# A whole second Strassen level in the first down product, and the snapshots' additions moved from VectorE to ScalarE and GpSimd

## The chip, the cores and the metric

The kernel runs on one core of one Trainium2 chip. The metric is device time in microseconds (us), the median of several runs. One further execution was taken by the hardware profiler; "the profile" and "the trace" are of that execution. The engines are named as in the profile: PE is TensorE's matrix multiplication, PEld its weight load, DVE is VectorE, ACT is ScalarE, POOL is GpSimd, SP is SyncE, which issues most of the transfers.

## What is computed

A transformer block on 2048 tokens of 1024 values, in bf16: linear attention with 32 heads of 32, then a feed-forward network with a ReLU gate. Both work on a normalised input and are added to what came in.

```python
h  = x  + linear_attention(layernorm(x), wqkv, wo)      # wqkv 1024 x 3072, wo 1024 x 1024
n  = layernorm(h)
gate = n @ W_gate                                       # 1024 x 3584
up   = n @ W_up                                         # 1024 x 3584
h2 = h + ((gate * (gate > 0)) * up) @ W_down            # 3584 x 1024
```

## The kernel before

**Order of the work.** The program text does not issue instructions. An object `Plan` records every operation, with the parts of memory that it reads and writes, and then sorts the operations of each engine by a list schedule with fixed costs and due times (`schedule`); the result is one fixed order per engine. Each engine works its own queue in order and waits at an instruction whose inputs are not ready, with everything behind it. As all operations are issued by one line (`call` in `Plan.take`, line 122), every row of the profile shows L122, and operations are told apart by shapes and times.

**Strassen products.** The large products are done in the Strassen-Winograd form: a product of 2 x 2 blocks takes seven block products instead of eight, with sums of the blocks made on DVE beforehand and additions of partial results afterwards. `Quad` holds one such set of seven. It has three PSUM banks A, D and E. `p1` writes A, and a `fork` (an ACT copy from PSUM to PSUM) puts the same into D. `p6` is added to A, and a first snapshot `u2` of A is taken; `p5` goes to E; `p7` is added to A, and a second snapshot `u3` is taken; `p2` is added to D, which gives the result c11, and E with u3 gives c22; later `p4` on A gives c21, and `p3` on E, with u2, gives c12. `Quads.run` interleaves neighbours: the order on PE is p1, then p4 and p3 of the quad before, then p6, p5, p7, p2. So p3 writes bank E again after c22 has been read from it.

**The stages.** Attention comes first. Then the gate and up products with a first Strassen level (`gu_quad`, matmuls of 512 columns in pairs of banks); their results are the left matrices of the down product, partly kept in SBUF, partly spilled to DRAM (`l_dram`, `s_dram`). Sums of `W_down`'s blocks are made meanwhile and spilled to `r_dram` (`wd_sums`).

**The down stage** begins at 573.44 us. Its outer Strassen level has seven products m, done in the order 1, 2, 6, 5, 7, 3, 4; each product is 1024 tokens by 1792 by 512. `deep` does a product through a second, inner level: two quads, one for each half g of the tokens, each with seven inner products. An inner product has 2 token tiles x 7 steps = 14 matmuls of 256 columns. For this `inner_rights` makes four sums of the weights (t1, t2, t4, t3) and `inner_lefts` four sums of the left matrix for each g (s1, s2, s4, s3), DVE operations of 128x1792 in fp16. They are put into rings of fixed places in SBUF (`inner_r`, `inner_l`, in KB per partition). The quads use five banks, 0 to 4 (`deep_banks`).

The first product, m=1, is different in the kernel before: only half g=1 goes through the inner level. Half g=0 is done by `shallow`: plain accumulation over 14 steps with matmuls of 512 columns, four blocks in banks 5 to 7, each copied by ACT into the running results `UM`. Its right matrix `r1` is loaded during the gate stage in two halves of 896 KB (k = 0 and 1), and its left matrix `z1` in two pieces.

**Where results go.** `begin` starts the running results U from m=1. `plus` adds a product to a running result: it serves m=2, 6, 5, 3 and 4, ten quads in all. Its `usnap` takes both snapshots of the quad by one DVE addition straight from PSUM: bank A plus the running result goes to the new running result. `both`, for m=7, takes plain snapshots (`plain_snap`, an ACT copy to a scratch place from `m_ring`) and updates two running results, ten DVE additions for each quad. Finished parts are stored by POOL's queue, which adds them to what `out` already holds, or at the very end by SP's queue.

The functions that the change touches, and what calls them:

Of the kernel before, what the change touches and what calls it, by code (L numbers as in the profile page):

```python
# [9 lines left out]
ALU = mybir.AluOpType  # L10
FP32 = mybir.dt.float32
BF16 = mybir.dt.bfloat16
FP16 = mybir.dt.float16
# [435 lines left out]
def ring_of(items):  # L449
    n = [0]  # L450

    def take():
        n[0] += 1
        return items[(n[0] - 1) % len(items)]

    return take
# [3 lines left out]
def block_kernel(ctx: ExitStack, tc: tile.TileContext, x, wqkv, wo, wg, wu, wd, out, H: int):  # L460
    nc = tc.nc
    P = 128
# [11 lines left out]
    FH = FC // 2  # L474
# [24 lines left out]
    def at(kb, shape, dt=BF16):  # L499
        n = 1  # L500
        for v in shape:
            n *= v
        size = n * (2 if dt == FP32 else 1)
        lo = int(kb * KB)
        assert lo == kb * KB and lo + size <= MEM, (kb, shape)
        a = mem[:, lo:lo + size]
        if dt != BF16:
            a = a.bitcast(dt)
        if len(shape) == 2:
            a = a.rearrange("p (a b) -> p a b", b=shape[1])  # L510
        elif len(shape) == 3:
            a = a.rearrange("p (a b c) -> p a b c", b=shape[1], c=shape[2])
        elif len(shape) == 5:
            a = a.rearrange("p (a b c d e) -> p a b c d e", b=shape[1], c=shape[2], d=shape[3], e=shape[4])
        elif len(shape) == 4:
            a = a.rearrange("p (a b c d) -> p a b c d", b=shape[1], c=shape[2], d=shape[3])
        return a
# [15 lines left out]
    def bank(b, n=1):  # L533
        return psum[:, b, :] if n == 1 else psum[:, b:b + n, :]
# [13 lines left out]
    hw, nc = nc, Plan(nc)  # L548
# [219 lines left out]
    def v_quad(p):  # L768
        v = v_ring()

        def blk(i, j):
            return v[:, i, j * KH:(j + 1) * KH, 0:P]

        def copy(i, j):
            return lambda ps: nc.scalar.copy(out=blk(i, j), in_=split(ps))

        def add(i, j):
            return lambda ps, u: nc.vector.tensor_tensor(out=blk(i, j), in0=split(ps), in1=split(u), op=ALU.add)

        return v, Quad(tok_prod(p, WV), fork, snap,  # L780
                       {"c11": copy(0, 0), "c12": add(0, 1), "c21": copy(1, 0), "c22": add(1, 1)}, five_banks)
# [86 lines left out]
    for p in range(1, NP):  # L868
# [9 lines left out]
        v, vq = v_quad(p)  # L878
# [77 lines left out]
    o_ring = ring_of([at(180 + SH + 2 * i, [D]) for i in range(2)])  # L956
# [231 lines left out]
    order = [(0, fc) for fc in range(4)] + [(1, fc) for fc in (2, 3, 0, 1)]  # L1188
# [15 lines left out]
    DW = D // 2  # L1204
    DQ = D // 4
    FQ = FH // 2
# [22 lines left out]
    for n, (s, fc) in enumerate(order):  # L1229
# [18 lines left out]
        if n == 24:  # L1248
            r1 = at(164, [2, FQ, DW])
            for k in range(2):  # L1250
                nc.sync.dma_start(out=r1[:, k, :, :], in_=wd_pairs[:, 0, :, k, 0:DW])
            z1 = l1_part(0, 12)
# [8 lines left out]
    lq = [at(84, [FQ, 4, 2, SW])[:, :, q, :, :] for q in range(4)]  # L1261
# [1 line left out]
    lx = at(0, [FQ, 2, SW], FP16)  # L1263
    L0 = {1: lq[0], 2: lq[1], 3: lf[1], 4: lq[3], 5: lx, 6: lf[0], 7: lf[2]}
    z_kb, r_kb = ring_of([14, 28]), ring_of([42, 164])
    inner_r, inner_l = ring_of([150.5, 178]), ring_of([0] + [140, 72] * 6)
    h_ring = ring_of([i for i in range(4)])
    o_ring = ring_of([190.5 + i for i in range(7)])
    m_ring = ring_of([197.5 + 2 * i for i in range(3)])
    UM = at(56, [NS, 2, 2, 2, DQ], FP32)  # L1270
    of_v = of.rearrange("(t p) d -> p t d", p=P)
    deep_banks = five([bank(b) for b in range(5)])
    shallow_bank = ring_of([bank(b) for b in (5, 6, 7)])

    def U(s, v, g):
        return UM[:, s, g, v, :, :]

    def Y(s, v, g):
        n = (2 * s + v) * 2 + g
        return at(84 + 8 * n if n < 7 else 188.5, [2, DQ], FP32)  # L1280

    def add(o, x, y):
        nc.vector.tensor_tensor(out=o, in0=x, in1=y, op=ALU.add)

    def pair(a):
        return a.rearrange("p (t d) -> p t d", t=2)
# [12 lines left out]
    def store(q, s, tt, lo, width, o, onto_h):  # L1299

        t = tile_no(q, s, tt)
        lo += q % 2 * DW
        dst = of_v[:, t:t + o.shape[1], lo:lo + width]
        if onto_h:
            nc.gpsimd.dma_start(out=dst, in_=o, accum_op=ALU.add)
        else:
            nc.sync.dma_start(out=dst, in_=o)
# [21 lines left out]
        for f in range(FQ):  # L1329
            nc.sync.dma_start(out=L0[m][:, f, :, :], in_=s_dram[m][:, 2 * f:2 * f + 2, :])  # L1330

    def shallow(m, r, lefts, order, then, tts=range(4)):
        for s in order:
            for tt in tts:
                b = shallow_bank()
                for f in range(FH):
                    if f == FH - 1:
                        nc.cut()
                    nc.tensor.matmul(b, lhsT=lefts[s][f][:, tt * P:(tt + 1) * P], rhs=r[:, f % 2, f // 2, :],
                                     start=(f == 0), stop=(f == FH - 1), skip_group_check=True)  # L1340
                then(s, tt, b)

    def inner_rights(r):
        y = [[r[:, k, :, v * DQ:(v + 1) * DQ] for v in range(2)] for k in range(2)]
        kb = inner_r()
        t1, t2, t4 = (at(kb + 3.5 * i, [FQ, DQ], FP16) for i in range(3))
        t3 = y[0][1] if r.dtype == FP16 else None
        if t3 is None:
            t3 = y[0][1].bitcast(FP16)
        for o, a, b in ((t1, y[0][1], y[0][0]), (t2, y[1][1], t1), (t4, y[1][0], t2), (t3, y[1][1], y[0][1])):  # L1350
            nc.vector.tensor_tensor(out=o, in0=a, in1=b, op=ALU.subtract)
        return y[0][0], y[1][0], y[1][1], t4, t1, t2, t3
# [26 lines left out]

        return of(x00), of(x01), of(s4), x11, of(s1), of(s2), s3.get  # L1380

    def deep(m, r, x1, outs, gs=range(2)):

        rights = inner_rights(r)

        def quad(g):
            lefts = inner_lefts(L0[m], x1[g], g)

            def prod(ps, k, start):
                for tt in range(2):  # L1390
                    for f in range(FQ):
                        nc.tensor.matmul(ps[:, tt * DQ:(tt + 1) * DQ], lhsT=lefts[k - 1](f)[:, tt * P:(tt + 1) * P],
                                         rhs=rights[k - 1][:, f, :], start=(start and tt == 0 and f == 0),
                                         stop=(f == FQ - 1), skip_group_check=True)

            usnap, end = outs(g)
            return Quad(prod, fork, usnap, {
                "c11": lambda D: end(0, 0, D, None), "c21": lambda A: end(1, 0, A, None),
                "c12": lambda E, u: end(0, 1, E, u), "c22": lambda E, u: end(1, 1, E, u)}, deep_banks)

        for g in gs:
            quads.run(quad(g))

    def plus(src, dst=None, q=None, last=False):


        def outs(g):
            with_h = last and g == 1

            def base(s, v):  # L1410
                x = src(s, v, g)
                if with_h:
                    add(x, x, load_h(q, s, 2 * g, 2, v * DQ, DQ))
                return x

            def usnap(A, which):
                b = base(which, 1)
                o = dst(which, 1, g)
                add(o, pair(A), b)
                return o  # L1420

            def end(s, v, ps, u):
                x = base(s, v) if u is None else u
                if q is None:
                    add(dst(s, v, g), pair(ps), x)
                else:
                    o = at(o_ring(), [2, DQ])
                    add(o, pair(ps), x)
                    store(q, s, 2 * g, v * DQ, DQ, o, not with_h)

            return usnap, end

        return outs

    def plain_snap(A, which):
        u = scratch_u()
        nc.scalar.copy(out=u, in_=pair(A))
        return u

    def seven(s, tt, b):  # L1440
        for v in range(2):
            y = U(s, v, tt // 2)[:, tt % 2, :]
            add(y, b[:, v * DQ:(v + 1) * DQ], y)
        o = at(o_ring(), [1, DW])
        for v in range(2):
            c = slice(v * DQ, (v + 1) * DQ)
            add(o[:, 0, c], b[:, c], Y(s, v, tt // 2)[:, tt % 2, :])
        store(3, s, tt, 0, DW, o, True)

    def begin(g):  # L1450

# [28 lines left out]
    def step(m, outs):  # L1480
        deep(m, right(m), left(m), outs)


    shallow(1, r1, ([lq[0][:, f // 2, f % 2, :] for f in range(FH)], [z[:, f, :] for z in z1 for f in range(z.shape[1])]), (1, 0),
            lambda s, tt, b: nc.scalar.copy(out=UM[:, s, 0, :, tt, :], in_=b.rearrange("p (v d) -> p v d", v=2)), (0, 1))
    z1 = [z.rearrange("p (j u) t -> p u j t", u=2)[:, :, :, 2 * P:] for z in z1]
    deep(1, r1, {1: [(lo, lo + z.shape[2], z[:, 0, :, :], z[:, 1, :, :]) for lo, z in zip((0, 6), z1)]}, begin, (1,))

    step(2, plus(U, scratch_u, q=0))
    left0(5)  # L1490

# [5 lines left out]
    r, z = right(7), left(7)  # L1497
    deep(7, r, z, both)

    o_ring = ring_of([*(4 + i for i in range(10)), *(190.5 + i for i in range(7))])  # L1500
# [54 lines left out]
```

## Time and profile before

| | us |
|---|---|
| median of 3 runs | 730.73 (730.35 to 730.91) |
| profiled execution, its own time | 730.03 |
| its span in the trace | 728.2 |
| start of the down stage on PE | 573.44 |
| end of the last matmul | 724.78 |
| busy in the span: PE | 715.6 |
| DVE | 557.7 |
| ACT | 278.8 |
| POOL | 80.3 |

The span runs from the first to the last event in the trace; 1.83 us of the profiled execution lie around it. Matrix products fill the span almost wholly: PE is busy for 98% of it. After the last matmul a single addition and a store of 1.81 us follow. Times in the trace are counted from the start of the span.

### The profile page before, as it was taken

What the parts mean: (1) busy time and instruction counts of PE and PEld (TensorE: products, weight loads), DVE (VectorE), ACT (ScalarE), POOL (GpSimd) and SP (SyncE); (2) the same over time, 40 slices, a digit from 0 to 9 for tenths busy, and PEclk for the clock granted to TensorE, in tenths of its full rate; (3) what the DMA queues carried; (4) which work ended last, traced back from release to release, by engine and by line L of the source; (5) the groups of instructions that cost most, each with busy time, mean ns of one, the idle gap of its engine ahead of it and who ended that gap; (6) DMA issues with size and microseconds to landing.
All of it is one profiled execution on the core that took longest, in us unless ns stands there. A gap on an engine that the chain in (4) does not pass through costs nothing.

```text
span 728.2 us, 11123 instructions
## 1 busy us (share of the span) xinstructions
PE 715.6 (98%) x4121; PEld 391.7 (54%) x4121; DVE 557.7 (77%) x941; ACT 278.8 (38%) x543; POOL 80.3 (11%) x90
## 2 busy tenths in 40 slices
PE   8999999999999999999999999999999999999998
PEld 3444545444444444444444444444444488888887
DVE  6997635896897785575767969769766869899996
ACT  5778545666555443333333333333333220001100
POOL 2433000002202120000000000000000004101452
PEclk9999999999999999999999999999999999999999
DMA  9955205239946730456156485675591878867974
GB/s 308 240 125 115 38 1 173 60 84 239 198 102 151 143 83 1 123 145 181 58 145 200 151 252 159 190 242 186 161 292 59 287 244 222 247 223 230 246 81 61
DMA packets 156503, 117.40 MB, mean 161 GB/s; under 512 B 54944, under 2 KB 140192, under 8 KB 156320
## 3 DMA queue, kind: packets, MB, share of 16 engines
q1 hardware_dynamic: 148832, 113.01, 54.5%
q0 software_dynamic: 7616, 3.67, 4.9%
q8 instruction: 32, 0.52, 0.3%
q14 instruction: 23, 0.19, 0.1%
HBM read 70.52 MB, written 34.08 MB: 144 GB/s over the span
## 4 chain that ended last, share of the span: by engine, by line
PE 86%; DVE 5%; ACT 3%; DMA 3%; issue 1%; POOL 0%; SPq 0%; ACTq 0%; DVEq 0%
PE psum L122 86%; DVE mem L122 4%; ACT mem L122 3%; DMA mem<-mem 3%; DVE tiny L122 1%; POOL mem L122 0%; DMA mem<-in_A_x_dram 0%; ACT tiny L122 0%; SPq L122 0%; ACT psum L122 0%; ACTq L122 0%; DVEq L122 0%
## 5 line engine op out<-in xcount | busy, mean ns | idle before, releaser
L122 PE MATMUL psum<-mem 128*128 128x512 f16 (+4 forms) x4105 | 714.5, 337 | 7.9 <-ACT mem L122 3.5
L122 PEld LDWEIGHTS <-mem 128*128 128x128 f16 (+1 forms) x4121 | 391.7, 98 | 332.8 <-issue 8.2
L122 DVE TENSOR_TENSOR mem<-psum,mem 128x512 f32<-128x512 f32 (+2 forms) x238 | 186.0, 794 | 108.9 <-ACT mem L122 71.1
L122 DVE TENSOR_TENSOR mem<-mem 128x512 f16<-128x512 bf16 (+8 forms) x394 | 237.1, 642 | 13.5 <-DMA mem<-mem 8.1
L122 ACT COPY mem<-psum 128x512 f32<-128x512 f32 (+2 forms) x124 | 92.6, 749 | 216.7 <-PE psum L122 212.8
L122 ACT COPY psum<-psum 128x512 f32<-128x512 f32 (+1 forms) x67 | 48.5, 725 | 157.6 <-PE psum L122 143.2
L122 POOL DMA_DIRECT2D out_dram<-mem x28 | 34.1, 1299 | 415.1 <-DVE mem L122 415.0
L122 POOL TENSOR_SCALAR mem<-mem,tiny 128x1024 bf16<-128x1024 bf16 x30 | 39.6, 1320 | 196.5 <-ACT tiny L122 174.0
L122 ACT ACTIVATE mem<-psum 128x512 bf16<-128x512 f32 x90 | 53.8, 598 | 16.9 <-PE psum L122 16.3
L122 DVE SCALAR_TENSOR_TENSOR mem<-mem 128x512 bf16<-128x512 bf16 (+1 forms) x71 | 58.6, 825 | 1.4
L122 DVE SCALAR_TENSOR_TENSOR mem<-psum,mem 128x512 bf16<-128x512 f32 x66 | 45.3, 688 | 11.9 <-PE psum L122 7.9
L122 ACT ACTIVATE mem<-mem,tiny 128x1024 bf16<-128x1024 bf16 x25 | 28.6, 1145 | 10.8 <-issue 4.7
L122 DVE TENSOR_SCALAR mem<-mem 128x512 bf16<-128x512 bf16 (+1 forms) x49 | 16.4, 334 | 20.8 <-ACT mem L122 20.6
L122 ACT ACTIVATE mem<-mem 128x1024 bf16<-128x1024 f32 (+1 forms) x24 | 25.3, 1055 | 5.9 <-DVE mem L122 5.9
L122 DVE TENSOR_TENSOR mem<-psum,tiny 128x384 bf16<-128x384 f32 (+1 forms) x48 | 22.9, 508 | 5.3 <-ACT tiny L122 3.9
L122 ACT ACTIVATE tiny<-tiny 128x1 f32<-128x1 f32 (+2 forms) x112 | 22.7, 206 | 9.1 <-DVE tiny L122 6.2
L122 ACT ACTIVATE tiny<-psum 128x12 f32<-128x12 f32 (+1 forms) x48 | 8.1, 169 | 13.8 <-PE psum L122 13.4
L122 ACT CAST mem<-psum 128x512 bf16<-128x512 f32 x18 | 10.5, 581 | 2.9 <-PE psum L122 2.2
L122 DVE BATCH_NORM_STATS2 tiny<-mem 128x6 f32<-128x512 bf16 x14 | 9.0, 678 | 2.4 <-DMA mem<-in_A_x_dram 2.4
L122 POOL TENSOR_SCALAR tiny<-tiny 128x1 f32<-128x1 f32 x14 | 5.1, 367 | 25.7 <-ACT mem L122 18.1
L122 ACT ACTIVATION_READ_ACCUMULATOR mem<-mem,tiny 128x1 f32 x25 | 4.7, 189 | 0.0
L122 DVE TENSOR_SCALAR tiny<-tiny 128x1 f32<-128x1 f32 x16 | 3.4, 210 | 0.3
(18 smaller groups left out, 13.5 us busy)
## 6 DMA issues: line engine op xcount, KB each, us to landing
l_dram<-mem SPq DMA_DIRECT2D x98, 128.0 KB, 2.2
mem<-l_dram SPq DMA_DIRECT2D x12, 896.0 KB, 6.5
mem<-in_A_x_dram SPq DMA_DIRECT2D x32, 256.0 KB, 3.0
mem<-in_B_W_up_dram SPq DMA_DIRECT2D x14, 512.0 KB, 5.2
mem<-in_B_W_gate_dram SPq DMA_DIRECT2D x14, 512.0 KB, 4.3
mem<-in_B_W_down_dram SPq DMA_DIRECT2D x28, 256.0 KB, 3.7
r_dram<-mem SPq DMA_DIRECT2D x56, 128.0 KB, 2.0
mem<-r_dram SPq DMA_DIRECT2D x8, 896.0 KB, 5.5
```

The costliest lines, as they stand in the source:

```text
L122: call = lambda: getattr(getattr(self.nc, eng), op)(*args, **k)
```

## The change

The half g=0 of the product m=1 goes through `deep` like the others, so that `shallow`, its banks and the unused function `seven` are gone, and `deep` loses its parameter for the halves. For this product the sums of the right matrix get their own three places in SBUF (188, 196 and 199.5 KB), which are free before the gate stage ends, and those of the left matrix a place more in their ring. The scratch ring `m_ring` lies elsewhere during m=1.

Independent of that, `usnap` in `plus` now takes each snapshot in two steps: an ACT copy from PSUM to a scratch place, and a POOL addition of that copy and the running result. There are 20 such snapshots.

```diff
-    inner_r, inner_l = ring_of([150.5, 178]), ring_of([0] + [140, 72] * 6)
+    inner_r = ring_of([(188, 196, 199.5)] + [tuple(kb + 3.5 * i for i in range(3)) for kb in (150.5, 178)] * 3)
+    inner_l = ring_of([0, 140, 0, 72] + [140, 72] * 5)
...
-    m_ring = ring_of([197.5 + 2 * i for i in range(3)])
+    m_ring = ring_of([178, 180, 182, 184])
...
-    shallow_bank = ring_of([bank(b) for b in (5, 6, 7)])
...
-    def shallow(m, r, lefts, order, then, tts=range(4)):
-        for s in order:
-            for tt in tts:
-                b = shallow_bank()
-                for f in range(FH):
-                    if f == FH - 1:
-                        nc.cut()
-                    nc.tensor.matmul(b, lhsT=lefts[s][f][:, tt * P:(tt + 1) * P], rhs=r[:, f % 2, f // 2, :],
-                                     start=(f == 0), stop=(f == FH - 1), skip_group_check=True)
-                then(s, tt, b)
-
     def inner_rights(r):
         y = [[r[:, k, :, v * DQ:(v + 1) * DQ] for v in range(2)] for k in range(2)]
-        kb = inner_r()
-        t1, t2, t4 = (at(kb + 3.5 * i, [FQ, DQ], FP16) for i in range(3))
+        t1, t2, t4 = (at(kb, [FQ, DQ], FP16) for kb in inner_r())
...
-    def deep(m, r, x1, outs, gs=range(2)):
+    def deep(m, r, x1, outs):
...
-        for g in gs:
+        for g in range(2):
             quads.run(quad(g))
...
             def usnap(A, which):
+                u = plain_snap(A, which)
                 b = base(which, 1)
                 o = dst(which, 1, g)
-                add(o, pair(A), b)
+                nc.gpsimd.tensor_tensor(out=o, in0=u, in1=b, op=ALU.add)
                 return o
...
-    shallow(1, r1, ([lq[0][:, f // 2, f % 2, :] for f in range(FH)], [z[:, f, :] for z in z1 for f in range(z.shape[1])]), (1, 0),
-            lambda s, tt, b: nc.scalar.copy(out=UM[:, s, 0, :, tt, :], in_=b.rearrange("p (v d) -> p v d", v=2)), (0, 1))
-    z1 = [z.rearrange("p (j u) t -> p u j t", u=2)[:, :, :, 2 * P:] for z in z1]
-    deep(1, r1, {1: [(lo, lo + z.shape[2], z[:, 0, :, :], z[:, 1, :, :]) for lo, z in zip((0, 6), z1)]}, begin, (1,))
-
+    z1 = [z.rearrange("p (j u) t -> p u j t", u=2) for z in z1]
+    deep(1, r1, [[(lo, lo + z.shape[2], z[:, 0, :, c], z[:, 1, :, c]) for lo, z in zip((0, 6), z1)]
+                 for c in (slice(0, 2 * P), slice(2 * P, 4 * P))], begin)
+
+    m_ring = ring_of([197.5 + 2 * i for i in range(3)])
     step(2, plus(U, scratch_u, q=0))
     left0(5)
```

More of the change, by code (lines that the diff above doesn't have):

```diff
@@ L1438, in plain_snap @@
         return u
[L1440 to L1448, printed above, removed]
     def begin(g):
```

## The prediction

> **What bounds the kernel now.** I read the page's busy table and its chain first, then the chain of waits of the last stage, that stage's windows and groups, and last the timelines of single engines.
>
> ```profile
> PE 715.6 (98%) x4121; PEld 391.7 (54%) x4121; DVE 557.7 (77%) x941; ACT 278.8 (38%) x543; POOL 80.3 (11%) x90
> PE 86%; DVE 5%; ACT 3%; DMA 3%; issue 1%; POOL 0%; SPq 0%; ACTq 0%; DVEq 0%
> ```
>
> TensorE (PE) is busy 98% of the span and owns 86% of the chain. The chain, cut to 540 to 730 us, is one entry:
>
> ```profile
> 539.93 184.85 PE psum L122 x1486
> 724.78 0.02 issue
> 724.81 0.69 DVE mem L122
> ```
>
> PE runs without a gap to 724.78, then one VectorE (DVE) addition and a store. The list of PE's waits from 540 us on is empty. So only PE's work, or a new wait of PE, moves the end. The down stage starts at 573.44. Its windows (start:end, length, then busy time and count of PE, weight loads, DVE, ACT, POOL; clock, DMA share, GB/s):
>
> ```profile
> 573.40:585.50 12.10, 12.10 (x57) 5.45 (x56) 11.76 (x14) 1.76 (x3) 0.00 (x0) 1.00 1.00 358
> 593.20:603.90 10.70, 10.70 (x101) 9.57 (x99) 8.40 (x10) 1.74 (x3) 0.00 (x0) 1.00 0.96 342
> 603.90:614.60 10.70, 10.70 (x101) 9.57 (x99) 9.97 (x13) 0.57 (x1) 5.02 (x4) 1.00 0.83 142
> 667.70:678.40 10.70, 10.70 (x100) 9.57 (x99) 10.63 (x16) 1.74 (x3) 3.61 (x3) 1.00 0.72 157
> ```
>
> PE is full in all four, and DVE is the next fullest engine (9.97 and 10.63 of 10.70), so what DVE can bear decides whether PE stays full. The stage's groups (busy, mean ns):
>
> ```profile
> L122 DVE TENSOR_TENSOR mem<-mem 128x1792 f16<-128x1792 f16 x52 | 55.1, 1084 | 0.2
> L122 DVE TENSOR_TENSOR mem<-psum,mem 128x512 f32<-128x512 f32 x46 | 31.5, 688 | 12.2 <-PE psum L122 6.5 <-ACT mem L122 4.9
> L122 ACT COPY mem<-psum 128x512 f32<-128x512 f32 x12 | 7.0, 586 | 30.2 <-PE psum L122 30.2
> L122 POOL DMA_DIRECT2D out_dram<-mem x28 | 34.1, 1299 | 415.1 <-DVE mem L122 415.0
> ```
>
> [...]halving the columns all but halves the price. The trace agrees: 109.1 and 215.9 ns, worked out below. [...]
>
> ```profile
> 221.27 1.28 POOL L122 TENSOR_SCALAR mem<-mem,tiny 128x1024 bf16<-128x1024 bf16 x1 [23.74 <-ACT tiny L122]
> 222.00 1.08 DVE L122 TENSOR_TENSOR mem<-mem 128x1024 f16<-128x1024 bf16 x1
> 226.93 1.19 POOL L122 TENSOR_SCALAR mem<-mem,tiny 128x1024 bf16<-128x1024 bf16 x1 [4.39 <-ACT tiny L122]
> ```
>
> Undisturbed, that DVE form takes 0.69 (70 of them average 0.698), so it lost 0.39; the POOL form takes 1.19 alone, 1.28 here, up to 1.71 elsewhere (at 184.03).
>
> **Part 1: the first product's token half g=0.** Removed: `shallow`, 4 blocks of 14 matmuls of 512 columns, evicted by four ACT copies:
>
> ```profile
> 576.66 0.59 ACT L122 COPY mem<-psum 128x512 f32<-128x512 f32 x1 [5.01 <-PE psum L122]
> 579.68 0.59 ACT L122 COPY mem<-psum 128x512 f32<-128x512 f32 x1 [2.44 <-PE psum L122]
> 605.60 0.57 ACT L122 COPY psum<-psum 128x512 f32<-128x512 f32 x1 [8.59 <-PE psum L122]
> 616.29 0.57 ACT L122 COPY psum<-psum 128x512 f32<-128x512 f32 x1 [10.13 <-PE psum L122]
> ```
>
> The first two starts lie 3.02 apart, 215.9 ns per matmul; 56 take 12.09. Added: one inner quad of 7 products x 14 matmuls of 256 columns. The two forks are one quad apart, 10.69 us, 109.1 ns each; 98 take 10.69 to 10.70. So PE saves 12.09 - 10.70 = **1.39 us**. As PE never waits, this is also the ceiling.
>
> ACT: less 4 copies, plus a fork, 2 snapshots and 2 evictions, +1; it is under a fifth full. DVE: 6 more left sums (four, two of them split because z1 is in two pieces), some 4 x 1.00 at back-to-back pitch, and 2 PSUM additions x 0.61: 5.2 us. The four right sums are only moved, t1 to t4 x 1.00 us, from after 575.6 into the gate stage, where the added ring slot (188, 196, 199.5) is free early. The built programs' orders place t1 in a DVE gap at 535.7 to 537.4, t3 and t4 in one at 554.3 to 557.4, and t2 in one at 550.23 to 551.20. Left sum s4 of g=0 is put between the gate stage's last two direct results (570.65 and 571.99), which pushes the second to about 573.0; DVE's last bank read there still starts near 573.65. Cover: PE's own gate products; price if it is gone, about 1 us each.
>
> SP issues the same 413 rows. r1's second half (896 KB) is issued ten places later, behind four `r_dram` stores, z1's load and two `l_dram` stores; it landed at 535.60 before, and by the rate of those queues I estimate 548.6 now, 1.6 us before t2 needs it. `left0(5)` waits longer for slot 0, but its pieces land at 613 to 617 and are needed by the product at about 635.
>
> New waits of PE: the first products need the bank whose last gate read ends at 574.87; PE gets to it at 574.97. After the first p1 only a half product (0.76) lies ahead of p6, and the fork needs 0.04 + 0.57 + 0.05 after a full one: about **0.06 us** of stall.
>
> **Part 2: the snapshots of m=2, 6, 5, 3, 4.** DVE loses 20 PSUM additions x 0.61 = 12.2 us. ACT gains 20 copies x 0.58. POOL gains 20 additions of 128x512 f32, a form that the trace of before does not have. The nearest row reads as many elements (1024 in one input): 1.19 us, which I take. [...] DVE per such quad: before 6 x 1.00 + 6 x 0.61 = 9.66, after 6 x 1.00 + 4 x 0.61 = 8.45 of 10.70. None of this is PE work, so nothing is won. POOL's queue holds the 28 accumulating stores too; the fullest quads (m=2 and 3) have four, 4 x 1.25 + 2 x 1.19 = 7.4 of 10.70. An addition behind a store starts up to 1.25 later, but the stores of a quad follow p2, p4 and p3, not p7, so I cost that at nothing for u3; u2, taken after p6, is not wanted before the next quad.
>
> The chain after p7 ends at T: ACT T+0.04 to 0.62, POOL T+0.75 to 1.94 (0.13 of semaphore), DVE's c22 addition T+1.97 to 2.66, then p3 may write that bank. p3's slot is T+4.43 (three products of 1.53 less the time between), so 1.7 us to spare; in the last quad nothing is interleaved, p3 is at T+2.90 and 0.2 to spare. In the first quad of m=3 DVE is still late from m=7's ten additions per quad (12.05 of 10.70): 0 to 0.3 of stall. I take **0.15** for all.
>
> **Sum.** 730.03 (the profiled execution, span 728.2 and 1.83 around it) - 1.39 + 0.06 + 0.15 = 728.85. The median shown is 0.70 above that execution: 729.55, so **729.5**. The least difference worth the name here is 0.2%, 1.46 us (729.27 and 732.19): the full gain lies just inside it.
>
> **Rivals.**
> (A) Slower: [...] If POOL's addition waits for a two-input DVE sum (1.00), [...]and one more such sum is ahead of c22 in DVE's queue, c22 ends at T+4.87, past T+4.43: 0.44 per quad. It decides from a chain of 4.43 us. [...] Nine quads x 0.44 = 4.0: 730.73 - 1.39 + 4.0 = 733.3. [...] Against: DVE waits in order at c22[...], and four additions read PSUM.
> (B) No change: the junction. If t2 waits for r1's late half, or s4 holds back the last gate bank by a whole sum, PE waits about 1 us: 730.3. For: t2's margin is an estimate and DVE's order is fixed. Against: other sums fill the gaps.
> (C) Faster by over 0.2%: no stall and a little scatter, 729.2 or less. Against: 1.39 is the ceiling.
> That the change doesn't do what it says is out: the built program has the 56 matmuls less and 98 more, and 20 additions on POOL.
>
> **How the numbers follow.** Forecast (small gain, within 0.2%) 0.42, B 0.12, C 0.26, A 0.20. Same is forecast and B, 0.54; faster 0.26; slower 0.20. The likeliest alone spans 729.1 to 730.1. For 8 in 10, I go from 728.9, which leaves out about 0.08, through B and into A, whose milder half (four quads, or 0.2 each) ends at 732.3, leaving out about 0.1.
>
> **What would show it.** Right: no 512-column matmul after the gate stage and 98 more of 256; PE unbroken to about 723.5; a POOL row of 20 additions near 1.2; DVE's busy time about 7 us less. Wrong: PE rows in the list of waits from 573 on. Behind p3, released by DVE with a POOL row at 1.5 or more and two-input sums well over 1.08, means A; at 550 to 576, released by DVE or ACT, means B. Should PE's pitch for 256 columns not be 109 beside POOL's work, my price of part 1 is wrong itself.

## The result, and the profile after

| | before | changed |
|---|---|---|
| median of 5 runs, us | 730.73 (730.35 to 731.0) | 734.1 (733.45 to 735.2) |
| ratio, 95% interval | | 1.005 (1.0036 to 1.0064) |
| profiled execution's span | 728.2 | 733.4 |
| last gate fork to the last matmul's end | 164.95 | 168.63 |

The change makes the kernel 3.4 us slower, where a gain of 1.2 us, to 729.5, was forecast. The last row of the table is used throughout. It runs from the start of the gate stage's last fork on ACT (559.83 before, 561.03 after) to the end of PE (724.78 and 729.66). In it the changed kernel loses 3.68. The 1.20 before it is not the change's: 1.09 of it is there at the first fork of all (23.45 and 24.54), before anything that was changed, and in the runs of this case that fork starts anywhere between 23.04 and 24.54. The profiled execution of the changed kernel, 735.2, is the longest of its five.

The page's busy times and the shares of its chain, changed kernel:

```profile
PE 715.0 (97%) x4163; PEld 396.2 (54%) x4163; DVE 563.6 (77%) x929; ACT 291.0 (40%) x564; POOL 109.9 (15%) x110
PE 83%; DVE 7%; DMA 4%; ACT 3%; issue 2%; POOL 1%; SPq 0%; POOLq 0%; ACTq 0%; DVEq 0%
```

DVE executes 12 operations less than before and yet is busy 5.9 us longer (563.6 against 557.7). PE's share of the chain fell from 86% to 83%, DVE's rose from 5% to 7%. PE's timeline from 540 us on (start, length, engine, operation, count, idle time before it and what ended it) and the list of PE's waits there (total, times, longest):

```profile
539.68 120.81 PE L122 MATMUL psum<-mem 128*128 128x512 f16 x946
662.23 32.26 PE L122 MATMUL psum<-mem 128*128 128x256 f16 x294 [1.73 <-DVE mem L122]
695.09 10.86 PE L122 MATMUL psum<-mem 128*128 128x256 bf16 x98 [0.61 <-DVE mem L122]
707.20 10.86 PE L122 MATMUL psum<-mem 128*128 128x256 bf16 x98 [1.25 <-DVE mem L122]
718.79 10.86 PE L122 MATMUL psum<-mem 128*128 128x256 f16 x98 [0.72 <-DVE mem L122]
```

```profile
PE psum L122 <- DVE mem L122: 4.3, 4, 1.7
```

Before, this was one stretch without a wait. Now there are four, all released by DVE and none before 660. Each begins about one product (1.53) after the start of a fork, that is, after the next quad's p1 and the old quad's p4, so it is the old quad's p3 that waits. In m=5 g=1, m=3 g=0, m=3 g=1 and m=4 g=0 it waits for the c22 addition, which frees bank E. The groups of the down stage show what DVE does meanwhile:

```profile
L122 DVE TENSOR_TENSOR mem<-mem 128x1792 f16<-128x1792 f16 x53 | 66.2, 1282 | 3.1 <-POOL mem L122 2.4 <-PE psum L122 0.4
L122 POOL TENSOR_TENSOR mem<-mem 128x512 f32<-128x512 f32 x20 | 32.8, 1668 | 358.0 <-ACT mem L122 348.2 <-issue 8.8 <-DVE mem L122 0.9
L122 DVE TENSOR_TENSOR mem<-psum,mem 128x512 f32<-128x512 f32 x28 | 18.7, 684 | 3.7 <-ACT mem L122 1.2 <-POOL mem L122 1.2 <-PE psum L122 1.0
```

DVE's long sums, with two inputs in SBUF, went from a mean of 1084 ns to 1282; its additions that read PSUM stayed at 684 (688 before). The profile counts what a sum gains in length as busy time (2.14 for 1.08 at 658.44, below), so longer busy time is not more work. The timeline of the worst place, m=5 g=1, where p7 ends at 655.96 (ACT, then POOL, then DVE):

```profile
652.94 0.58 ACT L122 COPY mem<-psum 128x512 f32<-128x512 f32 x1 [4.07 <-PE psum L122]
656.00 0.58 ACT L122 COPY mem<-psum 128x512 f32<-128x512 f32 x1 [2.47 <-PE psum L122]
...
656.41 3.22 POOL L122 TENSOR_TENSOR mem<-mem 128x512 f32<-128x512 f32 x2 [8.83 <-issue]
...
654.19 3.09 DVE L122 TENSOR_TENSOR mem<-mem 128x1792 f16<-128x1792 f16 x3
658.44 3.14 DVE L122 TENSOR_TENSOR mem<-mem 128x1792 f16<-128x1792 f16 x2 [1.16 <-POOL mem L122]
661.50 1.27 DVE L122 TENSOR_TENSOR mem<-psum,mem 128x512 f32<-128x512 f32 x2
```

Two things act here. The first is a wait that the built program sets, called W below. u2's copy is done at 653.52, but POOL's addition begins only at 656.41, because the program makes it wait for the second of the three sums; the sum at 658.44 waits for that addition in turn, and its 1.16 us of idle time is this wait. The reason is where things lie. In m=5 and m=3 the snapshots go to running results (`Y`) whose pieces of 2 KB stand in the gaps of a left matrix that these sums read with a stride. No byte is shared, but the program orders the two as if they overlapped. In the kernel before, DVE took the snapshots itself, and its own order was enough.

The second is that a DVE sum and a POOL addition take longer where they meet. u2's addition takes 2.00 instead of 1.26 beside the third sum. The sum at 658.44 takes 2.14 instead of 1.08 beside u3's addition, so that the two sums take 3.14 instead of 2.09. Only behind them, at 661.50, does c22 begin, whose input was there since 659.63. It ends at 662.18 and p3 starts at 662.23, 1.73 late.

Two sums in m=3 wait for POOL by W too, 1.23 and 1.16. The last of PE's four waits, in m=4 g=0, is without W and shows only the second (DVE, then POOL):

```profile
712.87 3.65 DVE L122 TENSOR_TENSOR mem<-mem 128x512 f32<-128x512 f32 x1
713.01 2.96 POOL L122 TENSOR_TENSOR mem<-mem 128x512 f32<-128x512 f32 x2
```

A DVE addition with both inputs in SBUF takes 3.65 instead of 0.68 while POOL's two additions run. c22, in the queue behind it, begins at 718.05, and PE waits 0.72.

### The profile page after: what moved, and what is told of

The parts are those of the page before. It is cut to its first block, busy times and chain, and to the rows that moved or that the text cites. A ratio compares the mean times of both kernels' runs of the same rounds, so it can differ in the third digit from the quotient of the medians.

```text
span 733.4 us, 11293 instructions
## 1 busy us (share of the span) xinstructions
PE 715.0 (97%) x4163; PEld 396.2 (54%) x4163; DVE 563.6 (77%) x929; ACT 291.0 (40%) x564; POOL 109.9 (15%) x110
## 4 chain that ended last, share of the span: by engine, by line
PE 83%; DVE 7%; DMA 4%; ACT 3%; issue 2%; POOL 1%; SPq 0%; POOLq 0%; ACTq 0%; DVEq 0%
PE psum L122 83%; DVE mem L122 6%; ACT mem L122 3%; DMA mem<-mem 2%; DMA mem<-in_A_x_dram 1%; POOL mem L122 1%; DVE tiny L122 0%; SPq L122 0%; ACT tiny L122 0%; ACT psum L122 0%; POOL out_dram L122 0%; POOLq L122 0%; ACTq L122 0%; DVEq L122 0%
## 5 line engine op out<-in xcount | busy, mean ns | idle before, releaser
L122 PEld LDWEIGHTS <-mem 128*128 128x128 f16 (+1 forms) x4163 | 396.2, 98 | 333.1 <-issue 13.7
L122 DVE TENSOR_TENSOR mem<-mem 128x512 f16<-128x512 bf16 (+8 forms) x400 | 255.1, 680 | 20.4 <-DMA mem<-mem 8.0
L122 DVE TENSOR_TENSOR mem<-psum,mem 128x1024 bf16<-128x1024 f32 (+2 forms) x220 | 172.7, 802 | 101.0 <-ACT mem L122 64.7
L122 ACT COPY mem<-psum 128x512 f32<-128x512 f32 (+2 forms) x144 | 104.4, 726 | 280.1 <-PE psum L122 271.0
L122 POOL TENSOR_TENSOR mem<-mem 128x512 f32<-128x512 f32 x20 | 32.8, 1668 | 358.0 <-ACT mem L122 348.2
```

Of the source, the lines that this page charges most:

```text
L122: call = lambda: getattr(getattr(self.nc, eng), op)(*args, **k)
```

## The experiments

Two theories stood against each other. **L**, the lock: POOL's additions and DVE's two-input sums exclude each other; DVE falls late; c22 stands behind sums in DVE's fixed queue; PE waits. "Lock" is a name for the longer operations on both sides (2.14 for 1.08 on DVE, 2.00 for 1.26 on POOL in m=5 g=1); what lies behind them no trace here shows. **H**, the hops: the longer chain ACT, POOL, DVE is too long by itself. A third, **J**, put the loss at the junction of the stages. **W**, the waits set by the program between DVE's sums and POOL's additions, has no experiment of its own. The kernels e3, e5 and e10 are without W on the sums, because POOL writes to other places there; e2, e6, e9, e11 and e12 have it. "Length" is the stretch from the last gate fork to PE's end, in the profiled execution.

| kernel | median | before, same job | ratio, 95% interval | length against before |
|---|---|---|---|---|
| e1, part 1 alone | 729.27 | 730.39 | 0.9988 (0.9976 to 0.9999) | -1.29 |
| e2, part 2 alone | 738.51 | 730.39 | 1.0114 (1.0099 to 1.013) | +7.65 |
| e5, quarter-wide POOL additions | 729.0 | 730.39 | 0.9976 (0.9964 to 0.9989) | -1.29 |
| e10, POOL additions nobody reads | 733.71 | 730.39 | 1.0043 (1.003 to 1.0056) | +3.41 |
| e3, the wait for POOL taken away | 735.32 | 730.58 | 1.0074 (1.0054 to 1.0093) | +4.80 |
| e6, u2 alone moved | 730.12 | 730.58 | 0.9995 (0.9987 to 1.0004) | -0.45 |
| e7, u3 alone moved | 730.75 | 730.58 | 1.0005 (0.9993 to 1.0017) | +0.22 |
| e11, e2 with early right sums | 737.01 | 730.58 | 1.0094 (1.0077 to 1.011) | +6.34 |
| e14, POOL only writes | 729.39 | 730.64 | 0.9983 (0.9976 to 0.999) | -1.29 |
| e12, plan prices the lock | 732.03 | 730.64 | 1.0019 (1.0011 to 1.0028) | +2.19 |
| e9, plan prices POOL | 738.37 | 730.64 | 1.0108 (1.0093 to 1.0123) | +8.88 |

### e1: part 1 alone

```diff
             def usnap(A, which):
-                u = plain_snap(A, which)
                 b = base(which, 1)
                 o = dst(which, 1, g)
-                nc.gpsimd.tensor_tensor(out=o, in0=u, in1=b, op=ALU.add)
+                add(o, pair(A), b)
                 return o
```

> Only part 1: the whole m=1 product through the inner level, the snapshots of m=2, 6, 5, 3, 4 taken by DVE straight from PSUM as before. Theory L (the lock: POOL's additions and DVE's two-input sums exclude each other, DVE falls late, and its c22 addition, queued behind sums, makes PE wait at p3) and theory H (the longer chain ACT, POOL, DVE alone, as it is ordered in DVE's queue) both put the whole loss on part 2: 730.7 - 1.3 = 729.4, no wait of PE at any p3. Theory J (the junction to the down stage costs what part 1 gains): 730.5 or more, and waits of PE between 573 and 595.

Measured 729.27, 0.12% faster than before; this is the fastest complete version here. PE's timeline is one entry again, and the sums have their old length:

```profile
539.75 184.36 PE L122 MATMUL psum<-mem 128*128 128x512 f16 x1528
```

```profile
L122 DVE TENSOR_TENSOR mem<-mem 128x1792 f16<-128x1792 f16 x53 | 56.2, 1082 | 0.4
```

The length is 1.29 less, so 0.1 of the 1.39 is lost; all of it before the fork at 594, that is, at the junction. J falls, and the whole loss belongs to part 2.

### e2 and e11: part 2 alone, and with early right sums

e2 is the kernel before with the new `usnap`. e11 adds to it the ring of places from part 1:

```diff
-    inner_r, inner_l = ring_of([150.5, 178]), ring_of([0] + [140, 72] * 6)
+    inner_r = ring_of([(188, 196, 199.5)] + [tuple(kb + 3.5 * i for i in range(3)) for kb in (150.5, 178)] * 3)
...
-    m_ring = ring_of([197.5 + 2 * i for i in range(3)])
+    m_ring = ring_of([178, 180, 182, 184])
```

(`m_ring` goes back to its old places after m=1, as in the changed kernel.)

> Only part 2: the snapshots by ACT and POOL, m=1 half by plain accumulation as before. L and H: the loss of the changed kernel without its gain of 1.3, 734.1 + 1.3 = 735.4 (735.0 to 736.0), with PE's waits at p3 in m=5, 3 and 4. If the harm arises only when both parts stand together: 731 or less.

> As e2 (part 2 alone, 738.5, of which PE's first waits come as early as m=2), with one piece of part 1 added: m=1's right sums get the places that are free early, so that DVE makes three of the four in the gate stage. If e2 is 3.6 worse than parts 1 and 2 together would say because DVE enters m=2 with its right sums still to do: 735 to 736.5, without waits of PE in m=2. If that reason is wrong: 738.5.

e2 lost 8.1, not 4.7: part 2 is worse alone than beside part 1, where it costs 4.5 (3.4 lost and 1.1 not gained). The waits of PE, e2 first, then e11:

```profile
PE psum L122 <- DVE mem L122: 6.5, 6, 1.4
```

```profile
PE psum L122 <- DVE mem L122: 5.5, 5, 1.4
```

Of e2's six waits, one (1.01 at 618) lies in m=2, where the changed kernel has none. With three of m=1's right sums made early it goes, and the loss falls to 6.4. So the head start that part 1 gives DVE is worth 1.7 of the 3.6 by which e2 exceeds the sum of the parts; the other 1.9 is not explained. Part of it stands in a wait of 0.85 in m=5 g=0, which the changed kernel has not, and in one of 1.32 instead of 0.72 in m=4 g=0.

### e5 and e10: the chain with a short lock, and the lock without the chain

e5 keeps ACT's copy, POOL's step and c22's wait, with a quarter of the elements; the plan's price of the step is pinned to the old one.

```diff
-                o = dst(which, 1, g)
-                nc.gpsimd.tensor_tensor(out=o, in0=u, in1=b, op=ALU.add)
-                return o
+                c = (slice(None), 0, slice(0, P))
+                nc.gpsimd.tensor_tensor(out=u[c], in0=u[c], in1=b[c], op=ALU.add)
+                return u
```

> As the changed kernel, with each POOL addition only 128 of 512 elements wide (three quarters of the base's addition are left out, and the sum is written over the copy); ACT's copy, POOL's step and DVE's wait for it stay, and the plan counts POOL's step at its old price so that DVE's order stays nearly the same. L: [...]DVE loses a quarter to a third and c22 ends before p3: 729.5, at most 730.3. H: the chain keeps its hops and its place in DVE's queue, PE still waits: 733 or more.

As POOL writes over the copy, W is gone from the sums too. e10 is e1 with additions on POOL beside it:

```diff
                 add(o, pair(A), b)
+                nc.gpsimd.tensor_tensor(out=at(161.5, [2, DQ], FP32), in0=o, in1=o, op=ALU.add)
                 return o
```

> As e1 (DVE takes the snapshots from PSUM), with 20 POOL additions of 128x512 f32 besides that read the snapshot and write a place that nobody reads (extra work, nobody waits for it). L: the additions still shut DVE's two-input sums out for up to 1.2 us each; DVE's 9.66 of 10.70 us per quad become up to 12.0, so PE waits again at p3: 732 to 740. H: nobody waits for POOL, so the time is that of e1, 729.4.

In e5 PE's timeline has no wait, and the length is e1's to the hundredth. POOL's row and DVE's sums in e5:

```profile
L122 POOL TENSOR_TENSOR mem<-mem 128x128 f32<-128x128 f32 x20 | 16.2, 809 | 369.2 <-DMA mem<-s_dram 329.9 <-ACT mem L122 39.2
L122 DVE TENSOR_TENSOR mem<-mem 128x1792 f16<-128x1792 f16 x53 | 58.6, 1139 | 2.6 <-PE psum L122 2.2
```

The shortest of POOL's steps take 0.44 and 0.45 there; longer ones, up to 1.69, bring the mean to 0.81. In e10 nobody reads what POOL writes, and PE waits all the same:

```profile
PE psum L122 <- DVE mem L122: 3.4, 6, 0.8
```

```profile
L122 DVE TENSOR_TENSOR mem<-mem 128x1792 f16<-128x1792 f16 x53 | 61.3, 1178 | 0.4
```

H falls by both: the hops without the long lock cost nothing, the lock without the hops costs 4.4 over e1. e5 alone does not tell L from W, for it is without both; e10 does.

PE's six waits in e10 do not stand at p3, as was expected, but at p7 (five) and p4. There PE needs bank A, which DVE reads too late, because DVE takes the snapshots itself and they stand behind stretched sums. So e10 shows L by another wait than the changed kernel's. Four of DVE's additions in m=6 and m=5 do wait for POOL, 0.93 each, as they overwrite what POOL still reads; five of PE's six waits come over 25 us after the last of these.

### e3, e6 and e7: how much the wait for POOL adds

e3 leaves the changed kernel's POOL work in place and lets c12 and c22 take ACT's copy:

```diff
-                o = dst(which, 1, g)
-                nc.gpsimd.tensor_tensor(out=o, in0=u, in1=b, op=ALU.add)
-                return o
+                nc.gpsimd.tensor_tensor(out=at(161.5, [2, DQ], FP32), in0=u, in1=b, op=ALU.add)
+                return u
```

> As the changed kernel, but POOL's additions write a place that nobody reads, and DVE's c12 and c22 take ACT's copy instead (the base of these two results is left out). The lock stays, the wait for POOL's result goes; the plan may now put c22 further ahead in DVE's queue. If what hurts is DVE's time lost to the lock (e10 has 20 additions that nobody waits for and lost 4.4): DVE needs 8.45 + 2 x 1.15 = 10.75 of 10.70 us per quad and stays late, 731 to 734. If the wait for POOL's result is needed for the harm, as in the changed kernel, where c22 had 8.45 us of DVE work and two more hops: 729.3, as e1.

It is slower than the changed kernel, and above the range given for L. There is a single wait of PE, of 4.19 us, and the timeline shows it whole (DVE, POOL, then PE):

```profile
697.13 8.55 DVE L122 TENSOR_TENSOR mem<-mem 128x1792 f16<-128x1792 bf16 x5
705.61 1.27 DVE L122 TENSOR_TENSOR mem<-psum,mem 128x512 bf16<-128x512 f32 x2
...
698.40 4.33 POOL L122 TENSOR_TENSOR mem<-mem 128x512 f32<-128x512 f32 x2
...
706.34 23.01 PE L122 MATMUL psum<-mem 128*128 128x256 bf16 x196 [4.19 <-DVE mem L122]
```

Five sums stand ahead of c22 in DVE's queue. They would take 5.0; with two POOL additions among them they take 8.55. c22's input, ACT's copy, was ready at 698.23; it starts at 705.61 without depending on POOL at all, and none of the sums waits for POOL by W. This is the clearest single picture of L.

A part of e3's loss comes after the wait: TensorE's granted clock (the column after PE's count) falls to a half for some 3 us.

```profile
706.30:709.30 3.00, 2.96 (x15) 0.50 0.39 40
709.70:710.00 0.30, 0.30 (x6) 1.00 1.07 94
```

The 196 matmuls behind the wait take 23.01, where two quads in a row take 21.4 elsewhere. Less these 1.6 us, e3's length would be about as much above the kernel before (3.2) as that of the changed kernel (3.68). In the changed kernel, whose longest wait is 1.73, the clock stays at 1.00.

e6 and e7 move one snapshot of the two, which each halves POOL's work:

```diff
-                nc.gpsimd.tensor_tensor(out=o, in0=u, in1=b, op=ALU.add)
+                if which == 0:                       # e7: which == 1
+                    nc.gpsimd.tensor_tensor(out=o, in0=plain_snap(A, which), in1=b, op=ALU.add)
+                else:
+                    add(o, pair(A), b)
```

> As the changed kernel, with only the first snapshot of each quad (u2, wanted a quad later) on ACT and POOL, the second (u3) by DVE from PSUM. DVE needs 6 x 1.00 + 5 x 0.61 = 9.05 plus 1.15 for one locked addition = 10.2 of 10.70. If lateness of DVE by the lock rules: within its slack, 729.3 to 730.0. If u2's late addition, which keeps POOL from u3, was the trouble: also as e1, 729.3.

> As the changed kernel, with only the second snapshot (u3, which c22 waits for) on ACT and POOL, u2 by DVE from PSUM. DVE again 10.2 of 10.70. If DVE's lateness alone rules: as e6, 729.3 to 730.0. If the wait of c22 for POOL is a cause of its own: slower than e6, 730.5 to 732, with waits of PE at p3 in m=5, 3 or 4.

e6 gives up over half of part 1's gain, e7 all of it: one wait of 0.68 in e6, two of 0.21 and 0.49 in e7. e6, at 730.12, lies just above its range. e7, at 730.75, lies in the range given for c22's wait as a cause of its own; but it is only 0.6 above e6 and their intervals overlap, so whether that wait adds something is not settled. In the length, u2's addition alone costs 0.84 over e1 and u3's alone 1.51; both together cost 4.97, over twice the sum. That DVE still has slack with one addition per quad would explain this, but is not shown.

### e14: writes in place of POOL's additions

```diff
                 add(o, pair(A), b)
+                spare = at(161.5, [2, DQ], FP32)
+                nc.scalar.copy(out=spare[:, 0, 0:1], in_=pair(A)[:, 0, 0:1])
+                nc.gpsimd.memset(spare, 0.0)
                 return o
```

> As e10 (e1, with extra work on POOL that nobody waits for, +4.4), but POOL's 20 additions are replaced by 20 memsets of 128x512 f32, which only write; an ACT copy of one column ahead of each sets its time. If it is POOL's reading from SBUF that shuts DVE's two-input sums out[...]: the sums keep 1.08 us and the time is that of e1, 729.3. If any use of SBUF by POOL does it, or POOL's activity as such: the sums stretch in proportion to the memset's length, and with a memset of about 1 us 732 to 734.

```profile
L122 POOL MEMSET mem<- 128x512 f32 x20 | 10.4, 522 | 375.3 <-ACT mem L122 375.2
L122 DVE TENSOR_TENSOR mem<-mem 128x1792 f16<-128x1792 f16 x53 | 56.3, 1086 | 0.4
```

Twenty writes of the same size leave the sums at 1086 ns and the time at e1's. But this tests less than was meant. A memset starts with DVE's own snapshot from PSUM, not after it, so that only four of the 20 run beside a long sum (in e10, 15 of the 20 additions run beside a DVE operation with two inputs in SBUF). One of the four, DVE and then POOL:

```profile
694.58 1.09 DVE L122 TENSOR_TENSOR mem<-mem 128x1792 f16<-128x1792 f16 x1
695.05 0.52 POOL L122 MEMSET mem<- 128x512 f32 x1 [0.48 <-ACT mem L122]
```

The memset lies inside the sum, and neither is longer than alone; the other three sums take 1.08 to 1.09 too. In these four cases POOL's writing did not lengthen DVE's sum; that the time stays at e1's says little.

### e12 and e9: the same work in another order

Both leave every operation as it is in the changed kernel and alter only the prices by which the plan orders the queues.

```diff
 # e12: a long two-input sum on DVE
-            return n / (0.96 * mode) + 69 + acc, 95 + self.SEM
+            return n / (0.96 * mode) + 69 + acc + (380.0 if n >= 1536 and narrow else 0.0), 95 + self.SEM
 # e9: an addition on POOL, 0.69 us in the plan so far
-        return n * 1.15 + 100, 60 + self.SEM
+        return (2400.0, 160.0) if eng == "gpsimd" and op == "tensor_tensor" else (n * 1.15 + 100, 60 + self.SEM)
```

> The changed kernel with the same work, but the plan prices each of DVE's long two-input sums 0.38 us higher (2 x 1.15 us of lock spread over 6 sums per quad), so that it sees DVE nearly full and orders the queues by that. If the place of c22 behind two to four sums in DVE's fixed order is what turns the lock into a wait of PE: the waits at p3 shrink to a third or less, 729.5 to 731. If DVE simply lacks the time (8.45 + 2.3 = 10.75 of 10.70 per quad): 733 or more, with the waits elsewhere.

> The changed kernel with the same work, but the plan prices POOL's addition at 2.4 us instead of 0.69. It then knows how late u3 is, though not that DVE's sums are stretched. If POOL's price in the plan is the fault: 729.5 to 731. If it is DVE's lost time that the plan doesn't know: c22 goes still further back among the sums, 734 or more.

The waits of PE, e12 first:

```profile
PE psum L122 <- DVE mem L122: 2.6, 4, 1.3
```

```profile
PE psum L122 <- DVE mem L122: 7.6, 5, 2.1
```

Order alone moves the time from 732.0 to 738.4. e12 fell between its two expectations: the place of c22 among the sums is a part of the loss, of which better prices take back some 2 of 4.8 us (734.1 against e1's 729.3; 1.5 of 5.0 in the length), not nearly all. With e9 the plan knows how late POOL's result is, but not that DVE's sums stretch, and the waits grow from 4.3 to 7.6. In e9's trace the granted clock also falls to about a half from 664.5 to 668, after a wait of 2.14, and the 294 matmuls behind that wait take 33.92 instead of 32.26. This is the longest of e9's four executions; two of the others, at 737.7 and 737.8, had a mean clock of 1.00.

## Why the prediction was wrong

**Part 1** was right. Of the 1.39, 1.29 arrived: 0.1 is lost at the junction, where 0.06 was reckoned. t1 to t4 ran in the gaps of the gate stage as described (t2 at 551.35), and r1's second half landed at 547.9, 3.5 before t2, so that rival B never arose.

**Part 2** was wrong in one term of the sum: the stalls, put at 0.15, were 4.31 in four waits. With what PE loses around each they cost 5.0: the 98 matmuls after a wait take 10.86 instead of 10.69, and the fork after the first wait comes 12.60 after the one before it. And 5.0 - 1.29 is the 3.7 of the table. Four steps led there.

- "DVE waits in order at c22" was the argument against rival A. DVE does wait in order, but c22 is not next: up to three sums stand between p7's end and c22 in its queue. The time of DVE's chain, T+2.66, holds only where c22 comes next; it did so in the last quad, which ended at T+2.69. In the others c22 ended at T+3.0 to T+6.2. The count of 6 sums and 4 additions per quad gave DVE's load, not its order, and e12 and e9 show what the order is worth.
- "8.45 of 10.70" left the lock out. Each of the 20 additions took DVE some 0.7: e1's DVE time less 20 additions of 0.688 is 562.6 - 13.8 = 548.8, and 563.6 was measured, 14.8 more. In the stage's groups it is 11.1 on the long sums (89.5 against 78.4 in e1) and 3.0 on a single addition, the one of 3.65 in m=4 g=0.
- u2's addition was costed at nothing since nobody wants it before the next quad. But it is ahead of u3 in POOL's queue. Where it is held up, as from 653.5 to 657.3 (by W and then beside a sum), both additions fall together on the critical chain. In m=3 g=0 a store stood ahead of u3, one of m=7's, late because DVE was late; this had been ruled out by looking only at the quad's own stores. u3's addition then still waited for a DVE sum by W, to 693.06.
- W has no term at all. The three sums that wait for u2's addition stand ahead of c22 and idle for 3.55 us in all. In three of the four waits of PE, W and the lock act together, and how they share the 3.59 us of these is not shown. That the lock alone can cost as much is what e3 and e10 show.

The price of POOL's addition itself was good: 1.26 where nothing disturbs it, for 1.19 taken; the mean of 1668 ns contains longer ones, such as the one of 2.00. Rival A had an addition of POOL that waits for a sum and a sum ahead of c22, and nearly the time, 733.3. The time is in part luck: it came from 0.44 in each of nine quads and not from 0.6 to 1.7 in four, and W was not in it. Its T+4.87 also rests on a length of POOL's addition that was only the author's assumption; with the 1.26 measured here in its place it is T+4.78, 0.35 per quad and 732.5. The range ended at half of A.

DVE's busy time was to fall by 7 and rose by 5.9. The test that was named for rival A was met: waits behind p3, released by DVE, POOL's row above 1.5, sums well over 1.08.

## What to carry to other kernels

In this kernel an operation moved from DVE to POOL was not off DVE: each addition of 1.26 us, which reads SBUF, took some 0.7 from DVE's two-input operations, and this shows as longer operations, not as waits. A move can also bring new waits between the two queues where their operands only lie among each other (1.16 to 1.23 us each here): read in the built program what each waits for. What counts in a fixed queue is not an engine's load but what stands ahead of the one operation that the bottleneck waits for (in m=5 g=1 c22, its input there since 659.63, began at 661.50 behind two sums), so read the order of that queue behind the critical point before calling a load harmless. The two parts should be kept apart: part 1 alone is faster than the kernel before, by 0.12% (0.01 to 0.24).

## What was unexpected of the hardware

The lengthening goes both ways. In m=4 g=0 two additions of POOL (1.75 and 1.73 instead of 1.26) ran one after the other while a single DVE addition lasted, 3.65 us instead of 0.68; in m=5 g=1 POOL's addition took 2.00 instead of 1.26 beside a DVE sum. On neither engine does the profile name a cause: the time appears as a longer instruction. The idle times at the same place, 8.83 put down to "issue" on POOL and 1.16 released by POOL on DVE, are waits for inputs or set by the program, and not a part of this.

Two waits of PE cost more than their own length: after 4.19 us in e3, and after 2.14 in e9, the granted clock stood at about a half for some 3 us, which cost another 1.6 us or so. After the waits of up to 1.73 in the changed kernel it did not fall.
